# Linear attention into a two-layer network: w_in loaded in 128-row blocks, units 8 to 15 of the first tile worked block by block, and v's casts and part of q's normalisation moved to other engines

## The chip, the cores and the metric

The kernel runs on one core of a Trainium2 chip. The metric is device time in microseconds: the median of the runs, and beside it one profiled execution whose trace is read here. The engines are called TensorE (PE), VectorE (DVE), ScalarE (ACT), GpSimd (POOL) and SyncE (SP); each works through its own instructions in order and waits on semaphores for the others. DMAs are issued by SP (the hardware queue) and by POOL (the software queue, which casts f32 to bf16 on the way).

## The reference

Inputs q, k, v are (8, 8, 576, 64): batch, heads, sequence, head size. The weights are w_in (512 x 2048) and w_out (2048 x 512), all f32.

```python
q_s = softmax(q, axis=-1)            # over the 64 of a head
k_s = softmax(k, axis=2)             # over the sequence
kv  = einsum('bhsd,bhse->bhde', k_s, v)
x   = einsum('bhsd,bhde->bhse', q_s, kv)      # -> (4608 tokens, 512)
h   = x @ w_in                       # 4608 x 2048
out = maximum(0.01 * h, h) @ w_out   # 4608 x 512
```

## The kernel before

A batch has 4608 / 8 = 576 tokens. On load, one partition holds 9 consecutive rows of a head pair's sequence (R = 9; L = 64 partitions make a head), with HL = 4 such groups side by side, so a raw tile is 128 x 4 x 9 x 64 f32. `RA` are rows 0 to 3, `RB` the rest; `R1` and `R2` cut RB for the first batch. For a batch the kernel finds k's maximum over the sequence, subtracts it and takes exp (`k_tree`, `k_sub`, `k_exp`), casts v to bf16 with a column of ones (`v_cast`), multiplies both on PE (`kv`, `kv_pair`; the ones column gives the softmax denominator), and scales the result into the block-diagonal `kd`. q is shifted, exponentiated and normalised (`q_sub`, `q_exp`, `q_sum`, `q_norm`), turned on PE or by a DMA (`q_transpose`, `q_turn`), copied (`q_keep`) and multiplied by kd (`attend`) into `xT`, the network's input, turned: 4 blocks of 128 channels by 4608 tokens in bf16.

The network runs over 9 tiles of 512 tokens. Layer 1 has 16 units j per tile: a unit multiplies the 4 blocks of w_in for 128 of the 2048 inner channels with xT (`layer1`, block order 0, 2, 1, 3) and ScalarE applies the leaky function (`leaky`, into `gj`). Layer 2 (`layer2`) accumulates over the 16 blocks of w_out; `store` copies and writes out. Tile 0 is special: layer 1 goes in two halves of 256 tokens, the first half begun on units 0 to 7 with only blocks 0 and 2 (`begun`), because the x of blocks 1 and 3 is made meanwhile; its layer 2 walks j in the outer loop, 4 token groups in the inner.

The order of all engines' work is written out by hand (a manual schedule). Attention work of the next batch is hung between units with `at(tile, unit, functions)` and called by `run(tile, unit)`; units 0 to 15 are the first half's layer 1 of tile 0, 16 to 31 the second half's, 32 to 47 the w_out blocks of its layer 2.

Batch 0 at the start is written out separately. q's first four rows, k, v and q's remaining rows are loaded by SP in this order. `q_first` makes their maxima and, on ACT, 16 small exps with sums; the maxima of k go over PE (`k_max_pe`, `k_all_pe`) so that the subtraction `k_sub_ps` has one operand in PSUM. `wake(n)` puts n filler matmuls on PE.

Two kinds of lines order the transfers:

- A one-element GpSimd copy into `gate` that reads a tile holds back what is behind it on POOL's queue until that tile is there. Before, one gate on the last element of k (L516) stands ahead of the first half of w_in, another ahead of the second half (L542), behind k's last subtraction; a third (L572), on batch 1's k, stands ahead of w_out.
- `hold_sync(i, src)` (L511) is a tiny SP DMA from a corner of a weight tile; SP waits there until that piece of the weights has landed. Hold 0 stands ahead of batch 1's k, q, v; hold 1 ahead of batch 2's (`load_all(2)`).

`load_w_in(fh)` loads one half of w_in's columns with four DMAs from POOL; each takes 64 partitions for two blocks. `load_w_out` loads blocks of w_out, in pieces 0:2, 2:4, 4:8, 8:12 and 12:16.

PSUM has 6 banks under one tag for everything but the layer-2 outputs; a new tile takes a bank whose last reader is done.

Of the kernel before, what the change touches and what calls it, by code (L numbers as in the profile page):

```python
# [8 lines left out]
FP32 = mybir.dt.float32  # L9
# [10 lines left out]
L = 64  # L20
# [5 lines left out]
def kernel(  # L26
# [57 lines left out]

    ALLH, ALLR = slice(0, HL), slice(0, R)
    RA, RB = slice(0, 4), slice(4, R)
    R1, R2 = slice(4, 6), slice(6, R)
    st = [{} for _ in range(B)]


# [33 lines left out]


    w_in_r = moe_w_in.rearrange("(gg hp hh d) f -> gg hp d hh f", gg=2, hp=2, hh=2)
    w_in_t = w_in_sb.rearrange("p (hh gg) f -> p gg hh f", gg=2)

    def load_w_in(fh):
        fs = slice(fh * (F // 2), (fh + 1) * (F // 2))  # L130
        for gg in range(2):
            for hp in range(2):
                nc.gpsimd.dma_start(  # L133
                    out=w_in_t[hp * D : (hp + 1) * D, gg, :, fs], in_=w_in_r[gg, hp, :, :, fs]
                )

    w_out_r = moe_w_out.rearrange("(fb f) o -> f fb o", f=P)
# [11 lines left out]
    def k_tree(b, hs, steps=slice(0, 4)):  # L149
        n = hs.stop - hs.start  # L150
        ks = st[b]["k"][:, hs]
        if steps.start == 0:
            st[b]["t4"] = mx_pool.tile([P, HL, 4, D], FP32, name="t4")[:, 0:n]
        t4 = st[b]["t4"]
        t2, t1 = t4[:, :, 0:2], t4[:, :, 0]
        for o, i0, i1 in (
            (t4, ks[:, :, 0:4], ks[:, :, 4:8]),
            (t2, t2, t4[:, :, 2:4]),
            (t1, t1, t4[:, :, 1]),
            (st[b]["kmax"][:, hs], t1, ks[:, :, 8]),  # L160
        )[steps]:
            nc.vector.tensor_tensor(out=o, in0=i0, in1=i1, op=ALU.max)  # L162
# [46 lines left out]
    def v_cast(eng, b, gg):  # L209
        o = vb2[b % 2][:, :, gg, 0:128].rearrange("p r (h d) -> p h r d", h=2)  # L210
        i = st[b]["v"][:, 2 * gg : 2 * gg + 2]
        if eng is nc.scalar:
            eng.copy(out=o, in_=i)
        else:
            eng.tensor_copy(out=o, in_=i)  # L215
# [12 lines left out]
    def q_first(b, rs):  # L228

        n = rs.stop - rs.start  # L230
        st[b]["nmax"] = nmax = small_pool.tile([P, HL, n], FP32, name="nmax")
        qsum = small_pool.tile([P, n, HL], FP32, name="qsum")
        for hs in (slice(0, 2), slice(2, 4)):
# [12 lines left out]
        st[b]["qsum"] = qsum

    def q_first_rec(b, rs):
        n = rs.stop - rs.start
        st[b]["qrec", rs.start] = qrec = small_pool.tile([P, n, HL], FP32, name="qrec")  # L250
        nc.vector.reciprocal(out=qrec, in_=st[b]["qsum"])
# [25 lines left out]
    def q_norm(b, rs):  # L277
        n = rs.stop - rs.start
        qes = st[b]["qe"][:, rs]
        nc.vector.tensor_tensor(  # L280
            out=qes,
            in0=qes,
            in1=st[b]["qrec", rs.start].unsqueeze(3).to_broadcast([P, n, HL, D]),
            op=ALU.mult,
        )
# [256 lines left out]
    nc.gpsimd.tensor_copy(out=gate[:, 0:1], in_=st[0]["k"][:, HL - 1, R - 1, D - 1 : D])  # L542
    load_w_in(1)
    k_exp(0, H1)
    q_first_rec(0, RA)
    q_norm(0, RA)
    kv_pair(0, 0)
    wake(4)
    q_transpose(0, 0, 4)
    kv_pair(0, 1)  # L550
    for hh in range(2):
        kd_rec(0, 0, hh)
        kd_one(nc.vector, 0, 0, hh)
    q_keep(nc.scalar, 0, 0, 4, slice(0, 4, 2))
    q_keep(nc.vector, 0, 0, 4, slice(1, 4, 2))
    attend(0, [0, 2], 0, 256, nc.scalar)
    wake(3)
    kd_rec(0, 1, 0)
    kd_rec(0, 1, 1)
    kd_one(nc.vector, 0, 1, 0)  # L560
    kd_one(nc.vector, 0, 1, 1)
    q_max(0, R1)
    q_sub(nc.gpsimd, 0, R1)
    q_max(0, R2)
    q_sub(nc.gpsimd, 0, R2)
# [16 lines left out]
    at(0, 13, lambda: q_transpose(0, 6, 3), lambda: q_keep(nc.vector, 0, 6, 3))
    at(0, 15, lambda: attend(0, [0, 2], 256, 256, nc.scalar))
    at(0, 15, lambda: attend(0, [1, 3], 256, 256, nc.vector))
    at(0, 17, lambda: attend(0, [0, 1, 2, 3], 512, 64, nc.scalar))
# [3 lines left out]
    at(0, 15, lambda: q_max(1, RB), lambda: q_sub(nc.gpsimd, 1, RB))
    at(0, 29, lambda: k_exp(1, H1))  # L590
    at(0, 31, lambda: v_cast(nc.scalar, 1, 0), lambda: k_exp(1, H0))
    at(0, 33, lambda: q_exp(1, RA), lambda: q_sum(1, RA), lambda: q_norm(1, RA))
    at(0, 33, lambda: v_cast(nc.scalar, 1, 1), lambda: q_exp(1, RB), lambda: q_sum(1, RB))
# [58 lines left out]
    begun = []
    for j in range(0, 8, 2):
        ph = psB_pool.tile([P, 2, 256], FP32, name="ph", tag=BANK_TAG)
        for i in range(2):
            layer1(j + i, ph[:, i], 0, 256, slice(0, 2), i == 0)
        begun.append(ph)
    attend(0, [1, 3], 0, 256, nc.scalar)
    for half in range(2):
        for j in range(0, NF, 2):  # L660
            part = slice(2, 4) if begun else slice(0, 4)
            ph = begun.pop(0) if begun else psB_pool.tile([P, 2, 256], FP32, name="ph", tag=BANK_TAG)
            for i in range(2):
                layer1(j + i, ph[:, i], 256 * half, 256, part, i == 0, i == 1)
                if i == 1:
                    leaky(g_sb[j // 2][:, :, 256 * half : 256 * half + 256], ph)
                run(0, 16 * half + j + i)
# [65 lines left out]
```

## Time and profile before

| what | value |
|---|---|
| runs (3) | median 293.24 us, 293.17 to 293.56 |
| profiled execution | 293.27 us |
| its span, first to last instruction | 291.5 us |
| granted TensorE clock | 1.00 in every slice |
| PE busy | 280.2 us (96%) |
| DVE / ACT / POOL busy | 147.0 / 149.7 / 85.5 us |
| DMA, mean over the span | 157 GB/s; 45.76 MB |
| the chain that ended last | PE 89%, DMA 3%, DVE 1%, issue 1%, ACT 1%, POOL 1% |
| w_in pieces (8) | 256 KB each as written, 6.7 us median from issue to landing |
| w_out pieces (2 and 3) | 256 KB and 512 KB; 8.5 and 13.2 us from issue to landing |

The span is what lies between the first and the last instruction; the time is 1.8 us longer. A busy PE is not PE at its peak, because matmuls are pipelined: the view of the timeline gives the start of each group and, in brackets, the idle time before it with what ended it. In the timeline a line shows start, duration, engine, line of the kernel, operation, output and inputs, and xN for N merged instructions. Of a DMA the timeline shows only the issue; its landing is another figure. In the table by stretches each engine's busy time is followed by its instruction count, and the last columns are the granted clock, the share of the transfer engines and GB/s. The share can go over 1, because an engine's packets overlap.

### The profile page before, as it was taken

The numbers are of one execution on the slowest core, as the hardware profiler recorded it, in microseconds if no ns is written. First come the engines' busy times: TensorE is split into PE (matmuls) and PEld (weight loads), VectorE is DVE, ScalarE is ACT, GpSimd is POOL, SyncE is SP. The second block draws the span as 40 slices with busy tenths as digits, with TensorE's granted clock in tenths as the row PEclk, the third lists the DMA queues.
The fourth block names the chain that finished last, engine by engine and source line by source line (L and its number), as shares of the span: only waits on it lengthen the run. The fifth ranks groups of instructions, "written<-read, shape, count | busy, mean of one in ns | idle before, by whom it ended". The sixth has DMA issues, their size and how long they took to land.

```text
span 291.5 us, 4277 instructions
## 1 busy us (share of the span) xinstructions
PE 280.2 (96%) x1645; PEld 139.9 (48%) x1672; DVE 147.0 (50%) x244; ACT 149.7 (51%) x268; POOL 85.5 (29%) x61
## 2 busy tenths in 40 slices
PE   8697999999999999999999999999999999999995
PEld 3265845444544544454444544554455444444443
DVE  2947957896790796289276546645541200110011
ACT  4957683568168506941684339533953066017400
POOL 4545280008039208703910391029200000000000
PEclk9999999999999999999999999999999999999999
DMA  7999999597639454973299139913141310131032
GB/s 255 314 202 378 256 176 397 139 286 270 124 89 338 162 119 108 336 211 86 65 338 250 36 72 318 287 36 74 36 81 38 72 36 1 38 75 33 0 73 73
DMA packets 36580, 45.76 MB, mean 157 GB/s; under 512 B 15952, under 2 KB 19280, under 8 KB 36560
## 3 DMA queue, kind: packets, MB, share of 16 engines
q1 hardware_dynamic: 33120, 41.16, 48.4%
q0 software_dynamic: 3280, 4.20, 8.3%
q8 instruction: 13, 0.21, 0.3%
q10 hardware_dynamic: 160, 0.13, 0.1%
q14 instruction: 7, 0.06, 0.1%
HBM read 36.70 MB, written 9.44 MB: 158 GB/s over the span
## 4 chain that ended last, share of the span: by engine, by line
PE 89%; DMA 3%; DVE 1%; issue 1%; ACT 1%; POOL 1%; ACTq 0%
PE pout L479 43%; PE ph L458 41%; DMA w_in_sb<-in_moe_w_in_dram 3%; PE pkv L295 3%; PE po L446 2%; DVE k_raw L362 1%; PE psum_qt L395 1%; POOL w_in_sb L133 0%; ACT gj L467 0%; ACT xT L428 0%; PE po L418 0%; DVE out_sb L473 0%; POOL gate L542 0%; ACTq L467 0%
## 5 line engine op out<-in xcount | busy, mean ns | idle before, releaser
L479 PE MATMUL pout<-w_out_sb,gj 128*128 128x512 bf16 (+2 forms) x580 | 129.6, 373 | 0.6
L458 PE MATMUL ph<-xT,w_in_sb 128*128 128x512 bf16 (+1 forms) x626 | 126.8, 357 | 3.4 <-ACT xT L428 1.4
L467 ACT ACTIVATE gj<-ph 128x512 bf16<-128x512 f32 x144 | 82.5, 603 | 58.1 <-PE ph L458 57.5
L458 PEld LDWEIGHTS <-w_in_sb 128*128 128x128 bf16 x640 | 62.1, 98 | 64.8 <-issue 4.1
L479 PEld LDWEIGHTS <-gj 128*128 128x128 bf16 x592 | 57.0, 98 | 62.1 <-ACT gj L467 0.4
L473 DVE COPY out_sb<-pout 128x512 f32<-128x512 f32 (+1 forms) x34 | 22.7, 675 | 86.2 <-PE pout L479 80.7
L195 POOL TENSOR_TENSOR k_raw<-k_raw,kall 128x2304 f32<-128x2304 f32 (+1 forms) x6 | 29.1, 4846 | 83.5 <-DVE kall L187 56.3
L273 DVE TENSOR_REDUCE qsum<-qe 128x36 f32<-128x2304 bf16 (+4 forms) x11 | 19.8, 1799 | 37.4 <-ACT qe L264 37.4
L256 POOL TENSOR_TENSOR q_raw<-q_raw,qmax 128x2304 f32<-128x2304 f32 (+4 forms) x11 | 31.1, 2839 | 25.4 <-DVE qmax L226 25.4
L452 ACT CAST xT<-po 128x320 bf16<-128x320 f32 (+1 forms) x48 | 16.8, 402 | 41.2 <-PE po L446 41.2
L203 ACT ACTIVATE ke<-k_raw 128x2304 bf16<-128x2304 f32 (+2 forms) x11 | 17.6, 1596 | 10.3 <-POOL k_raw L195 8.6
L280 DVE TENSOR_TENSOR qe<-qe,qrec 128x2304 bf16<-128x2304 bf16 (+4 forms) x12 | 21.7, 1811 | 0.4
L226 DVE TENSOR_REDUCE qmax<-q_raw 128x36 f32<-128x2304 f32 (+4 forms) x11 | 19.4, 1789 | 0.0
L264 ACT ACTIVATE qe<-q_raw 128x2304 bf16<-128x2304 f32 (+4 forms) x11 | 16.9, 1533 | 0.8 <-POOL q_raw L256 0.8
L215 POOL CAST vb<-v_raw 128x1152 bf16<-128x1152 f32 x12 | 13.5, 1153 | 0.0
L324 PE MATMUL pout<-zero 128*128 128x512 bf16 x29 | 9.6, 470 | 1.5 <-POOL zero L101 1.3
L162 DVE TENSOR_TENSOR t<-k_raw 128x1024 f32<-128x1024 f32 (+1 forms) x10 | 10.1, 1011 | 0.5 <-DMA k_raw<-in_k_dram 0.2
L162 DVE TENSOR_TENSOR t<-t 128x256 f32<-128x256 f32 (+2 forms) x20 | 9.6, 478 | 0.7
L446 PE MATMUL po<-qX,kd 128*128 128x320 bf16 (+1 forms) x48 | 9.8, 286 | 0.0
L473 ACT COPY out_sb<-pout 128x512 f32<-128x512 f32 (+1 forms) x3 | 1.7, 563 | 14.9 <-PE pout L479 14.9
L295 PEld LDWEIGHTS <-ke 64*128 64x128 bf16 x252 | 7.2, 93 | 3.0 <-ACT gj L467 1.7
L313 DVE TENSOR_TENSOR kd<-pkv,krec 64x128 bf16<-64x128 f32 x28 | 8.1, 289 | 0.7
(57 smaller groups left out, 104.8 us busy)
## 6 DMA issues: line engine op xcount, KB each, us to landing
out_dram<-out_sb SPq DMA_DIRECT2D x70, 128.0 KB, 2.4
q_raw<-in_q_dram SPq DMA_DIRECT2D x7, 1152.0 KB, 8.4
v_raw<-in_v_dram SPq DMA_DIRECT2D x7, 1152.0 KB, 11.4
k_raw<-in_k_dram SPq DMA_DIRECT2D x6, 1152.0 KB, 6.1
k_raw<-in_k_dram SPq DMA_DIRECT2D x4, 576.0 KB, 5.7
w_in_sb<-in_moe_w_in_dram POOLq DMA_DIRECT2D x8, 256.0 KB, 6.7
w_out_sb<-in_moe_w_out_dram POOLq DMA_DIRECT2D x3, 512.0 KB, 13.2
v_raw<-in_v_dram SPq DMA_DIRECT2D x2, 576.0 KB, 7.7
```

The costliest lines, as they stand in the source:

```text
L162: nc.vector.tensor_tensor(out=o, in0=i0, in1=i1, op=ALU.max)
L195: eng.tensor_tensor(out=ks, in0=ks, in1=st[b]["kall"][:, hs].unsqueeze(2).to_broadcast([P, n, R, D]), op=ALU.subtract,)
L203: nc.scalar.activation(out=st[b]["ke"][:, :, hs].rearrange("p r h d -> p h r d"), in_=st[b]["k"][:, hs], func=AF.Exp,)
L226: nc.vector.tensor_reduce(out=m, in_=st[b]["q"][:, :, rs], axis=AX.X, op=ALU.max)
L256: eng.tensor_tensor(out=qs, in0=qs, in1=st[b]["qmax", rs.start].unsqueeze(3).to_broadcast([P, HL, n, D]), op=ALU.subtract,)
L264: nc.scalar.activation(out=st[b]["qe"][:, rs].rearrange("p r h d -> p h r d"), in_=st[b]["q"][:, :, rs], func=AF.Exp,)
L273: nc.vector.reduce_sum(out=qsum, in_=st[b]["qe"][:, rs], axis=AX.X)
L280: nc.vector.tensor_tensor(out=qes, in0=qes, in1=st[b]["qrec", rs.start].unsqueeze(3).to_broadcast([P, n, HL, D]), op=ALU.mult,)
L458: nc.tensor.matmul(ph, lhsT=w_in_sb[:, cb, j * P : (j + 1) * P], rhs=xT[:, cb, c0 : c0 + n], start=(i == 0 and first), stop=(i == NB - 1 a ...
L467: nc.scalar.activation(out=o, in_=ph, func=AF.Prelu, alpha=LEAKY_SLOPE)
L473: copy(out=out_sb, in_=pout)
L479: nc.tensor.matmul(pout, lhsT=g_sb[j // 2][:, j % 2, tsub * P : (tsub + 1) * P], rhs=w_out_sb[:, j, os], start=(j == 0), stop=(j == NF - 1),)
```

## The change

- Loads: `load_w_in` takes one 128-row block per DMA, in the order 0, 2, 1, 3 in which layer 1 uses them. The gate ahead of the second half reads `kmax` instead of the subtracted k, and v's two casts and the first normalisation now stand between that gate and the four DMAs on POOL's queue. Hold 0 reads block 2 instead of block 0. One w_out piece (0:2) goes ahead of the gate on batch 1's k, and 4:8 is cut into 4:6 and 6:8; all w_out loads and batch 2's loads are issued from the hook after unit 0.
- q of batch 0, rows 0 to 3: sums, reciprocals, normalisation, turn and copy by head pair. GpSimd normalises the first pair, VectorE the second. `attend` for blocks 0 and 2 is split in two, around the second kv product.
- q of batch 0, rows 4 to 8: rows 4 and 5 (R1), 6 and 7 (R2) earlier, with R1's normalisation on GpSimd and the turns between blocks of units 8 to 15; row 8 (R3) later, its turn and attend in layer 2 (units 35 and 38).
- Tile 0, first half: `begin` works a group of four bank pairs block by block and `end` finishes unit by unit. Units 0 to 7 begin with blocks 0 and 2, with blocks 1 and 3 of x made after block 0; units 8 to 15 with blocks 0, 2 and 1, and only block 3 is left to the unit loop.
- Batch 1's ScalarE work (exps and v's casts) stands at units 31 and 32 instead of 29 to 33. Filler matmuls go from 5, 4 and 3 to 3 and 3.

The core of the diff:

```diff
     def load_w_in(fh):
         fs = slice(fh * (F // 2), (fh + 1) * (F // 2))
         for gg in range(2):
-            for hp in range(2):
+            for hh in range(2):
                 nc.gpsimd.dma_start(
-                    out=w_in_t[hp * D : (hp + 1) * D, gg, :, fs], in_=w_in_r[gg, hp, :, :, fs]
+                    out=w_in_sb[:, 2 * hh + gg, fs], in_=w_in_r[gg, :, :, hh, fs]
                 )
...
+    def q_first_norm(eng, b, gg):
+        qes = st[b]["qe"][:, RA, 2 * gg : 2 * gg + 2]
+        eng.tensor_tensor(
+            out=qes,
+            in0=qes,
+            in1=st[b]["qrec2", gg].unsqueeze(3).to_broadcast([P, RA.stop, 2, D]),
+            op=ALU.mult,
+        )
...
     k_tree(0, H1, slice(1, 4))
+    nc.gpsimd.tensor_copy(out=gate[:, 0:1], in_=st[0]["kmax"][:, HL - 1, D - 1 : D])
+    v_cast(nc.gpsimd, 0, 0)
     k_max_pe(0, 1)
     wake(1)
     k_sub_ps(0, 0, HA)
     k_exp(0, slice(0, 1))
     k_all_dve(0, 1)
     k_all_pe(0, 1)
-    wake(5)
+    wake(3)
+    q_first_rec(0, 0)
+    q_first_norm(nc.gpsimd, 0, 0)
+    v_cast(nc.gpsimd, 0, 1)
     k_sub_ps(0, 0, HB)
     k_exp(0, slice(1, 2))
-    v_cast(nc.scalar, 0, 0)
-    v_cast(nc.scalar, 0, 1)
+    q_first_rec(0, 1)
+    load_w_in(1)
     k_sub_ps(0, 1)
-    nc.gpsimd.tensor_copy(out=gate[:, 0:1], in_=st[0]["k"][:, HL - 1, R - 1, D - 1 : D])
-    load_w_in(1)
     k_exp(0, H1)
-    q_first_rec(0, RA)
-    q_norm(0, RA)
     kv_pair(0, 0)
-    wake(4)
-    q_transpose(0, 0, 4)
+    q_turn_first(0, 0)
+    wake(3)
+    kd_rec(0, 0, 0)
+    kd_one(nc.vector, 0, 0, 0)
+    q_keep_first(nc.vector, 0, 0)
+    kd_rec(0, 0, 1)
+    kd_one(nc.vector, 0, 0, 1)
+    q_first_norm(nc.vector, 0, 1)
+    attend(0, [0], 0, 256, nc.scalar)
     kv_pair(0, 1)
+    attend(0, [2], 0, 256, nc.scalar)
+    q_turn_first(0, 1)
+    q_keep_first(nc.scalar, 0, 1)
...
-    hold_sync(0, w_in_sb[0:1, 0, F - 128 : F])
+    for rs in (R1, R2):
+        q_max(0, rs)
+        q_sub(nc.gpsimd, 0, rs)
+    hold_sync(0, w_in_sb[0:1, 2, F - 128 : F])
     st[1]["k"] = load(k, 1, "k_raw", [(H0, ALLR), (H1, ALLR)])
     st[1]["q"] = load(q, 1, "q_raw", [(ALLH, ALLR)])
     st[1]["v"] = load(v, 1, "v_raw", [(ALLH, ALLR)])
-    nc.gpsimd.tensor_copy(out=gate[:, 0:1], in_=st[1]["k"][:, 0, 0, 0:1])
-    for j0, j1 in ((0, 2), (2, 4), (4, 8), (8, 12), (12, 16)):
-        load_w_out(slice(j0, j1))
-    hold_sync(1, w_out_sb[0:1, 11, 0:128])
-    load_all(2)
+    def behind_first_units():
+        load_w_out(slice(0, 2))
+        q_max(0, R3)
+        q_sub(nc.gpsimd, 0, R3)
+        nc.gpsimd.tensor_copy(out=gate[:, 0:1], in_=st[1]["k"][:, 0, 0, 0:1])
+        for j0, j1 in ((2, 4), (4, 6), (6, 8), (8, 12), (12, 16)):
+            load_w_out(slice(j0, j1))
+        hold_sync(1, w_out_sb[0:1, 11, 0:128])
+        load_all(2)
...
+    at(0, 0, lambda: q_exp(0, R1), lambda: q_sum(0, R1), lambda: q_norm(0, R1, nc.gpsimd), behind_first_units)
+    at(0, 2, lambda: q_exp(0, R2), lambda: q_sum(0, R2), lambda: q_norm(0, R2))
+    at(0, 16, lambda: q_exp(0, R3))
+    at(0, 35, lambda: q_transpose(0, 8, 1), lambda: q_keep(nc.scalar, 0, 8, 1))
+    at(0, 38, lambda: attend(0, [0, 1, 2, 3], 512, 64, nc.scalar))
...
+    def begin(js, parts):
+        phs = [psB_pool.tile([P, 2, 256], FP32, name="ph", tag=BANK_TAG) for _ in js]
+        for i, between in parts:
+            for j, ph in zip(js, phs):
+                for h in range(2):
+                    layer1(j + h, ph[:, h], 0, 256, slice(i, i + 1), h == 0, False)
+            for fn in between:
+                fn()
+        return phs
...
+    def x1():
+        attend(0, [1], 0, 256, nc.scalar)
+        attend(0, [3], 0, 256, nc.vector)
+    t1 = (lambda: q_transpose(0, 4, 2), lambda: q_keep(nc.scalar, 0, 4, 2))
+    t2 = (lambda: q_transpose(0, 6, 2), lambda: q_keep(nc.vector, 0, 6, 2))
+    x2 = (
+        lambda: attend(0, [0, 2], 256, 256, nc.scalar),
+        lambda: attend(0, [1, 3], 256, 256, nc.vector),
+    )
+    for j0, parts in ((0, ((0, (x1,)), (1, ()))), (8, ((0, t1), (1, t2), (2, x2)))):
+        js = range(j0, j0 + 8, 2)
+        for j, ph in zip(js, begin(js, parts)):
+            end(j, ph, 0, slice(len(parts), 4), False)
+    for j in range(0, NF, 2):
+        end(j, psB_pool.tile([P, 2, 256], FP32, name="ph", tag=BANK_TAG), 1, slice(0, 4), True)
```

More of the change, by code (lines that the diff above doesn't have):

```diff
@@ L86 @@
     RA, RB = slice(0, 4), slice(4, R)
-    R1, R2 = slice(4, 6), slice(6, R)
+    R1, R2, R3 = slice(4, 6), slice(6, 8), slice(8, R)
     st = [{} for _ in range(B)]
@@ L126 @@
     w_in_r = moe_w_in.rearrange("(gg hp hh d) f -> gg hp d hh f", gg=2, hp=2, hh=2)
-    w_in_t = w_in_sb.rearrange("p (hh gg) f -> p gg hh f", gg=2)
     def load_w_in(fh):
@@ L231, in q_first @@
         st[b]["nmax"] = nmax = small_pool.tile([P, HL, n], FP32, name="nmax")
-        qsum = small_pool.tile([P, n, HL], FP32, name="qsum")
-        for hs in (slice(0, 2), slice(2, 4)):
+        for gg in range(2):
+            hs = slice(2 * gg, 2 * gg + 2)
+            st[b]["qsum", gg] = qsum = small_pool.tile([P, n, 2], FP32, name="qsum2")
             nc.vector.tensor_reduce(
@@ L236, in q_first, with q_first_rec, q_turn_first, q_keep_first @@
             )
-            for h in range(hs.start, hs.stop):
+            for h in range(2):
                 for r in range(n):
                     nc.scalar.activation(
-                        out=st[b]["qe"][:, rs.start + r, h],
-                        in_=st[b]["q"][:, h, rs.start + r],
+                        out=st[b]["qe"][:, rs.start + r, 2 * gg + h],
+                        in_=st[b]["q"][:, 2 * gg + h, rs.start + r],
                         func=AF.Exp,
-                        bias=nmax[:, h, r : r + 1],
+                        bias=nmax[:, 2 * gg + h, r : r + 1],
                         accum_out=qsum[:, r, h : h + 1],
                     )
[L246 to L251, printed above, removed]
+    def q_first_rec(b, gg):
+        st[b]["qrec2", gg] = qrec = small_pool.tile([P, RA.stop, 2], FP32, name="qrec2")
+        nc.vector.reciprocal(out=qrec, in_=st[b]["qsum", gg])
+    def q_first_norm(eng, b, gg):
[6 more added lines that the diff above has]
+        )
+    def q_turn_first(b, gg):
+        n = RA.stop
+        ps = psB_pool.tile([P, 2, n, L], BF16, name="psum_q2", tag=BANK_TAG)
+        for r in range(n):
+            nc.tensor.matmul(
+                ps[:, :, r],
+                lhsT=st[b]["qe"][:, r, 2 * gg : 2 * gg + 2].rearrange("p h d -> p (h d)"),
+                rhs=ident,
+                is_transpose=True,
+                start=(r == 0),
+                stop=(r == n - 1),
+            )
+        st[b]["ps2", gg] = ps
+    def q_keep_first(eng, b, gg):
+        o, i = st[b]["qT"][:, gg::2, RA], st[b]["ps2", gg]
+        if eng is nc.scalar:
+            eng.copy(out=o, in_=i)
+        else:
+            eng.tensor_copy(out=o, in_=i)
     def q_sub(eng, b, rs):
@@ L275, in q_sum, with q_norm @@
         nc.vector.reciprocal(out=qrec, in_=qsum)
-    def q_norm(b, rs):
+    def q_norm(b, rs, eng=nc.vector):
         n = rs.stop - rs.start
         qes = st[b]["qe"][:, rs]
-        nc.vector.tensor_tensor(
+        eng.tensor_tensor(
             out=qes,
@@ L535 @@
     k_all_pe(0, 1)
-    wake(5)
+    wake(3)
+    q_first_rec(0, 0)
+    q_first_norm(nc.gpsimd, 0, 0)
+    v_cast(nc.gpsimd, 0, 1)
     k_sub_ps(0, 0, HB)
     k_exp(0, slice(1, 2))
-    v_cast(nc.scalar, 0, 0)
-    v_cast(nc.scalar, 0, 1)
+    q_first_rec(0, 1)
+    load_w_in(1)
     k_sub_ps(0, 1)
-    nc.gpsimd.tensor_copy(out=gate[:, 0:1], in_=st[0]["k"][:, HL - 1, R - 1, D - 1 : D])
-    load_w_in(1)
     k_exp(0, H1)
-    q_first_rec(0, RA)
-    q_norm(0, RA)
     kv_pair(0, 0)
-    wake(4)
-    q_transpose(0, 0, 4)
+    q_turn_first(0, 0)
[7 more added lines that the diff above has]
+    attend(0, [0], 0, 256, nc.scalar)
     kv_pair(0, 1)
+    attend(0, [2], 0, 256, nc.scalar)
+    q_turn_first(0, 1)
+    q_keep_first(nc.scalar, 0, 1)
     for hh in range(2):
[L552 to L565, printed above, removed]
-    hold_sync(0, w_in_sb[0:1, 0, F - 128 : F])
+        kd_rec(0, 1, hh)
+        kd_one(nc.vector, 0, 1, hh)
+    for rs in (R1, R2):
+        q_max(0, rs)
+        q_sub(nc.gpsimd, 0, rs)
+    hold_sync(0, w_in_sb[0:1, 2, F - 128 : F])
     st[1]["k"] = load(k, 1, "k_raw", [(H0, ALLR), (H1, ALLR)])
@@ L582 @@
[L582 to L585, printed above, removed]
-    at(0, 15, lambda: k_begin(1), lambda: q_begin(1), lambda: k_tree(1, H0), lambda: k_tree(1, H1))
-    at(0, 15, lambda: k_allmax(1), lambda: k_sub(nc.gpsimd, 1, H0), lambda: k_sub(nc.vector, 1, H1))
-    at(0, 15, lambda: q_max(1, RA), lambda: q_sub(nc.gpsimd, 1, RA))
@@ L589 @@
[L589 to L593, printed above, removed]
+    def behind_first_units():
[7 more added lines that the diff above has]
+        load_all(2)
@@ new lines @@
+    at(0, 0, lambda: q_exp(0, R1), lambda: q_sum(0, R1), lambda: q_norm(0, R1, nc.gpsimd), behind_first_units)
[3 more added lines that the diff above has]
+    at(0, 38, lambda: attend(0, [0, 1, 2, 3], 512, 64, nc.scalar))
+    at(0, 15, lambda: k_begin(1), lambda: q_begin(1), lambda: k_tree(1, H0), lambda: k_tree(1, H1))
+    at(0, 15, lambda: k_allmax(1), lambda: k_sub(nc.vector, 1, H1), lambda: k_sub(nc.gpsimd, 1, H0))
@@ L594 @@
+    at(0, 16, lambda: q_sum(0, R3), lambda: q_norm(0, R3))
+    at(0, 16, lambda: q_max(1, RA), lambda: q_sub(nc.gpsimd, 1, RA))
+    at(0, 16, lambda: q_max(1, RB), lambda: q_sub(nc.gpsimd, 1, RB))
+    at(0, 31, lambda: k_exp(1, H1), lambda: k_exp(1, H0), lambda: v_cast(nc.scalar, 1, 0))
+    at(0, 32, lambda: q_exp(1, RA), lambda: q_sum(1, RA), lambda: q_norm(1, RA))
+    at(0, 32, lambda: v_cast(nc.scalar, 1, 1), lambda: q_exp(1, RB), lambda: q_sum(1, RB))
     at(0, 41, lambda: kv(1))
@@ L651, with end @@
     g_sb = g_tiles()
[L652 to L667, printed above, removed]
+    def begin(js, parts):
+        phs = [psB_pool.tile([P, 2, 256], FP32, name="ph", tag=BANK_TAG) for _ in js]
+        for i, between in parts:
+            for j, ph in zip(js, phs):
+                for h in range(2):
+                    layer1(j + h, ph[:, h], 0, 256, slice(i, i + 1), h == 0, False)
+            for fn in between:
+                fn()
+        return phs
+    def end(j, ph, half, part, first):
+        for h in range(2):
+            layer1(j + h, ph[:, h], 256 * half, 256, part, first and h == 0, h == 1)
+            if h == 1:
+                leaky(g_sb[j // 2][:, :, 256 * half : 256 * half + 256], ph)
+            run(0, 16 * half + j + h)
+    def x1():
[6 more added lines that the diff above has]
+        lambda: attend(0, [1, 3], 256, 256, nc.vector),
+    )
+    for j0, parts in ((0, ((0, (x1,)), (1, ()))), (8, ((0, t1), (1, t2), (2, x2)))):
[4 more added lines that the diff above has]
+        end(j, psB_pool.tile([P, 2, 256], FP32, name="ph", tag=BANK_TAG), 1, slice(0, 4), True)
     pout = [psO_pool.tile([P, O], FP32, name="pout") for _ in range(2)]
```

3 lines of the change are left out of this document (removed).

## The prediction, made before the changed kernel was run

> **What bounds the kernel now.** The page says TensorE (PE) is busy 280.2 of 291.5 us at full granted clock, so I looked only for time that PE loses. The chain of waits in order of time shows it at the front:
>
> ```profile
> 14.94 8.36 DMA w_in_sb<-in_moe_w_in_dram
> ...
> 23.44 1.69 PE ph L458 x14
> ...
> 36.41 8.37 PE pout L479 x38
> ...
> 53.30 2.10 PE ph L458 x9
> ```
>
> From 53.30 (tile 1) to 288 PE is busy 233.4 of 234.7 us by the busy table, and the diff touches nothing there. So the question is how much earlier than 53.30 tile 1 starts; that many us come off the total. The PE timeline shows what stands between:
>
> ```profile
> 17.37 1.91 PE L458 MATMUL ph<-xT,w_in_sb 128*128 128x256 bf16 x16
> 20.16 2.13 PE L458 MATMUL ph<-xT,w_in_sb 128*128 128x256 bf16 x18 [0.67 <-ACT xT L428]
> 23.44 1.69 PE L458 MATMUL ph<-xT,w_in_sb 128*128 128x256 bf16 x14 [1.15 <-DMA w_in_sb<-in_moe_w_in_dram]
> ```
>
> Unit 8 stops in its third block until the whole second half of w_in has landed (23.3). The busy table by stretches shows why that is late:
>
> ```profile
> 10.00:12.00 2.00, 1.67 (x11) 0.63 (x10) 2.00 (x5) 1.92 (x10) 0.84 (x2) 1.00 1.10 346
> ...
> 14.00:16.00 2.00, 1.82 (x31) 1.23 (x28) 1.29 (x5) 1.93 (x3) 1.57 (x3) 1.00 1.13 211
> ...
> 20.00:22.00 2.00, 1.84 (x17) 1.65 (x17) 0.00 (x0) 1.32 (x4) 0.59 (x1) 1.00 1.09 210
> 22.00:24.00 2.00, 0.85 (x9) 0.54 (x8) 1.50 (x3) 2.00 (x4) 0.00 (x0) 1.00 1.06 346
> ```
>
> The last two columns are the DMA share and GB/s: the transfer engines are full throughout, first with batch 0's q, k, v, then (about 205 GB/s written) with w_in, then with batch 1. The DMA records queue by queue put w_in's packets from 11.5 to about 22 without a gap, and batch 1 and w_out from 21.5 to 42.3. **So there are two clocks: PE's own work, and a transfer stream that is full to 42 us.** Who starts the stream's parts is in the SyncE and GpSimd timelines:
>
> ```profile
> 19.06 0.63 SPq L511 DMA_DIRECT2D held<-w_in_sb  x1
> 19.73 1.50 SPq L79 DMA_DIRECT2D k_raw<-in_k_dram  x2
> ...
> 40.62 0.52 SPq L511 DMA_DIRECT2D held<-w_out_sb  x1
> ```
>
> ```profile
> 8.28 2.57 POOL L133 DMA_DIRECT2D w_in_sb<-in_moe_w_in_dram  x4
> 13.08 0.19 POOL L542 COPY gate<-k_raw 128x1 f32<-128x1 f32 x1 [2.23 <-DVE k_raw L362]
> 13.20 2.38 POOL L133 DMA_DIRECT2D w_in_sb<-in_moe_w_in_dram  x4
> ...
> 69.79 2.24 POOL L215 CAST vb<-v_raw 128x1152 bf16<-128x1152 f32 x2
> ```
>
> The holds copy a corner of a landed piece, so their starts date landings: the fifth w_in piece at 19.0, w_out's blocks 8 to 11 at 40.6. From issue to landing, the other second-half pieces land at about 20.3, 21.7 and 23.3; w_out's pieces at 33.0, 35.1, 38.0, 40.6 and 43.1.
>
> **The change, part by part.**
>
> *v and q's first pair.* ScalarE loses two casts (2.20 us at 12.35). GpSimd is free of the first w_in issues at 10.85; gate 0.15, cast 1.12 (half of the 2.24 row) to 12.15, norm, cast. A bf16 normalisation on GpSimd is not in the trace; the nearest rows are its f32 subtraction of the same 512 elements (1.04 us) and VectorE's own normalisation of 512 (0.69). I take 1.04, and 0.69 to 2.1 (doubled) as ends. The second half's w_in issues then start at 14.4 (14.0 to 15.4), 1.2 us later than 13.20. The 0.69 normalisation of the second pair stays on VectorE at about 15.2, behind two scaled copies; one reciprocal (0.2) goes ahead of each k subtraction that follows, moving k's last exp from 14.45 to about 13.65, since ScalarE is free. The first kv product starts on k's second exp, about 12.75 instead of 13.54; the second on the last exp at 14.85 instead of 15.66. Two filler matmuls before and four after go (0.22 each), filling gaps only.
>
> *Units 0 to 7.* Attend 0, turn and keep of the second pair (0.35 + 0.6) and the copies of kd put the first layer-1 matmul at about 16.25 instead of 17.37. Sixteen matmuls, x1's two attends and the other 16 at 0.109 us are 3.9 us; blocks 3 and 4 landed by 17.8. Block 3 of x waits for VectorE, whose copy is now queued behind q's two maxima (0.68 each): 0.4 us. Units 0 to 7 end at 20.25 instead of about 22.1.
>
> *Units 8 to 15 by blocks.* Each block is 8 matmuls, 0.87 us: block 0 from 20.25 (landed 19.0; two pairs wait for ScalarE to free banks, whose queue has q's exps ahead of them) to 21.0; turn, block 2 (20.3) to 22.4; turn, block 1 (21.7) to 23.5; four attends to 23.95; block 3 (23.3) to 24.85. The q work inside costs PE what it cost before. First turn: GpSimd's normalisation of rows 4 and 5, issued behind the four w_in issues and two subtractions, is done at about 21.3, just covered; 0.5 us late costs 0.3. The second half's 64 matmuls take 6.95: layer 2 could start at 31.9, against 35.98, 4.1 us earlier. The row-8 turn and attend (0.25 + 0.28) now lie in layer 2, leaving 3.5.
>
> *The stream.* This is where the gain is cut. The blocks are 128 rows of 4 KB like the 64x2 before: same packets, no change taken (bounds none, since issue rows are 0.59 to 0.78 us for these 128 rows). The hold now waits for the sixth piece, 20.3 instead of 19.0, so k is issued at 21.0. SyncE's first packet came 1.8 us after its issue at 19.73, as w_in drained, and about 1 us after its issue at 0.74; I take 1.2, so batch 1 starts 0.3 us later than before (0 to 0.9). The w_out piece ahead of k, the gate and the extra issue (0.75; 6 issues for 5) only change the order: whatever the order, the piece with blocks 8 to 11 lands after all of batch 1 and 12 of 16 w_out blocks. So it lands at 40.6 + 0.3 = 40.9.
>
> *Layer 2.* Before, block 8's first matmul ran at 35.98 + 32 x 0.216 = 42.9 with 2.3 us in hand, and tile 1 began 10.4 us later (8 matmuls, kv of batch 1, turns, 24 matmuls, attends), unchanged in the new order. After, PE alone reaches block 8 at 31.9 + 6.9 + 0.5 = 39.3, and the piece lands at 40.9. Earlier waits (blocks 4 and 5 at about 36.3 against a need at 35.9) vanish in this one. v of batch 1 lands at 35 to 37; from there cast, exp, cast (1.14 + 1.06 + 1.14) fit before kv at 42.6. Tile 1 starts at 40.9 + 10.4 = 51.3: 2.0 us earlier.
>
> The profiled execution took 293.27 (span 291.5 plus 1.8), like the median of 293.24. **293.2 - 2.0 = 291.2 us.** Under 0.6 us, 0.2%, cannot be told from no change.
>
> **Rivals.**
>
> *The w_in stream gets a hole (about 292.6).* From the start of GpSimd's issue to the first packet passed 3.3 us at 8.28 and 3.8 at 25.23. If that is a fixed delay, pieces issued at 14.4 start at 17.7 to 18.2, while the first half runs out at 16.7: 1.0 to 1.5 us of nothing, and everything behind is as much later: 51.3 + 1.3 = 52.6, 292.5. Against it: both first packets came just when a batch transfer ran out (11.5: the last q rows; 29.0: q of batch 1), and the hardware queue's at 21.5 just when w_in did. So the delay looks like a turn awaited, with about 0.7 us in hand. [...]
>
> *GpSimd is slowed by VectorE and the kernel is slower (about 294).* In the trace GpSimd's 1152-element subtraction took 3.74 us beside VectorE's subtraction of the same size, half of the 5.07 us for twice the size being 2.5; and VectorE was held in turn:
>
> ```profile
> 34.89 3.74 POOL L195 TENSOR_TENSOR k_raw<-k_raw,kall 128x1152 f32<-128x1152 f32 x1 [5.95 <-DVE kall L187]
> ```
>
> ```profile
> 71.25 2.12 DVE L280 TENSOR_TENSOR qe<-qe,qrec 128x1280 bf16<-128x1280 bf16 x1
> ```
>
> (1.49 for that shape at 46.13; the two GpSimd casts ran until 72.0.) If the casts and norm run at half speed, 3.4 us become 6.8, the issue starts at 17.8, the stream stops for 2.8 us, and tile 1 starts at 54.1: 294.0. It decides from an issue at about 17. Against it: in that stretch VectorE subtracts with one operand in PSUM; the slow pairs have both in SBUF. [...]
>
> *PE is the only clock (289.8).* If the stream closes up where batch 1 and w_out alternate, tile 1 starts at 49.7 to 50.
>
> *The new order gives nothing*: only if PE's early start is fully lost in ScalarE's in-order queue; within the hole's result.
>
> **How the numbers follow.** Forecast 0.56 (own range 290.3 to 292.4), hole 0.15, slowed GpSimd 0.19, PE alone 0.10. The range goes from 289.7 to 294.0. Faster takes the forecast, PE alone and a little of the hole: 0.68. Same takes most of the hole, 0.13; slower 0.19.
>
> **What would show it.** Right: second w_in issue near 14.4 with DMA share full at 17 to 18, first layer-1 matmul near 16.3, layer 2 near 32, PE waiting on w_out before block 8 at about 41, tile 1 near 51.3. Wrong: issue after 16, a dip in GB/s at 17, PE waiting on kv of batch 1 instead of w_out, or a later stage that no longer starts as much earlier as tile 1 does.

## The result: 305.8 us, slower, and the profile after

The median went from 293.21 us to **305.81 us** (4 runs of each, 305.36 to 306.04 after), a ratio of 1.0425 with the interval 1.0407 to 1.0443. The profiled execution took 306.04 us, its span 304.3, its mean granted clock 0.981. The prediction, 291.2 with a range to 294.0, was wrong in size and in sign.

The forecast named the start of tile 1 as the figure that carries the time. That reading holds: tile 1 started at 53.30 before and starts at 66.07 now, 12.8 us later, and the time is 12.6 us longer. Everything lost is lost ahead of that point. Here is the PE timeline of the kernel after (start, duration, engine, line, operation; in brackets the idle time before and what ended it):

```profile
16.02 0.40 PE L264 MATMUL psum_q<-ident,qe 128*128 128x128 bf16 x4
22.17 1.89 PE L486 MATMUL ph<-xT,w_in_sb 128*128 128x256 bf16 x8 [5.75 <-DMA w_in_sb<-in_moe_w_in_dram]
...
44.99 1.89 PE L507 MATMUL pout<-w_out_sb,gj 128*128 128x512 bf16 x8 [2.32 <-DMA w_out_sb<-in_moe_w_out_dram]
...
53.01 0.28 PE L446 MATMUL po<-qT,kd 128*128 128x64 bf16 x4 [3.43 <-ACT qT L438]
53.12 4.43 PE L507 MATMUL pout<-w_out_sb,gj 128*128 128x512 bf16 x12
...
66.07 2.10 PE L486 MATMUL ph<-xT,w_in_sb 128*128 128x512 bf16 x9
```

PE was ready for layer 1 at 16.4, near the forecast 16.25, and then stood still for 5.75 us because the first piece of w_in was not there. Layer 2 waits once for w_out. The third large wait is at the row-8 attend, for a copy on ScalarE. The last number to see is 4.43 us for 12 matmuls that take 2.75 elsewhere. The busy table by stretches explains that, and the late w_in too (the last three columns are granted clock, DMA share, GB/s):

```profile
14.00:16.00 2.00, 1.95 (x27) 1.14 (x27) 1.78 (x6) 0.77 (x2) 2.00 (x3) 1.00 0.56 101
...
20.00:22.00 2.00, 0.00 (x0) 0.00 (x0) 0.00 (x0) 0.00 (x0) 0.25 (x1) 0.50 0.96 166
22.00:24.00 2.00, 1.83 (x9) 1.34 (x10) 0.00 (x0) 0.00 (x0) 0.00 (x0) 0.50 1.30 147
24.00:26.00 2.00, 2.00 (x12) 1.36 (x9) 1.15 (x3) 0.90 (x2) 0.00 (x0) 0.50 1.19 120
...
54.00:56.00 2.00, 2.00 (x6) 0.69 (x5) 1.93 (x3) 0.00 (x0) 0.00 (x0) 0.51 0.99 371
```

At 14 to 16 us, where w_in had the transfer engines to itself, they are half busy and move 101 GB/s; before it was 1.13 and 211. With the stops of 5.75 and 3.43 us the granted clock goes to half, from 19.9 to 26.7 us and from 54.0 to 57.4. Two more lines of the page, from the queues and from the DMA issues, say what is different about w_in:

```profile
q0 software_dynamic: 10464, 4.22, 9.8%
...
w_in_sb<-in_moe_w_in_dram POOLq DMA_DIRECT2D x8, 256.0 KB, 14.2
```

In the first line stand packets, MB and the share of the 16 engines' time. The software queue carried 3,280 packets before and 10,464 now, for the same 4.2 MB, and a piece takes 14.2 us to land where it took 6.7.

### The profile page after: what moved, and what is told of

Its sections match the earlier page's. It is cut to its first block, busy times and chain, and to the rows that moved or that the text cites. A ratio compares the mean times of both kernels' runs of the same rounds, so it can differ in the third digit from the quotient of the medians.

```text
span 304.3 us, 4299 instructions
## 1 busy us (share of the span) xinstructions
PE 284.7 (94%) x1666; PEld 140.8 (46%) x1666; DVE 148.1 (49%) x248; ACT 148.2 (49%) x270; POOL 92.6 (30%) x67
## 3 DMA queue, kind: packets, MB, share of 16 engines
q0 software_dynamic: 10464, 4.22, 9.8%
## 4 chain that ended last, share of the span: by engine, by line
PE 81%; DMA 8%; POOL 4%; DVE 3%; issue 1%; ACT 1%; SPq 1%; DVEq 0%
PE pout L507 40%; PE ph L486 37%; DMA w_in_sb<-in_moe_w_in_dram 5%; DMA k_raw<-in_k_dram 4%; PE pkv L323 3%; PE po L474 2%; POOL q_raw L284 1%; POOL w_in_sb L132 1%; DVE t L161 1%; POOL vb L214 1%; DVE k_raw L194 0%; ACT qe L292 0%; DVE qmax L225 0%; PE psum_qt L423 0%; SPq L79 0%
## 5 line engine op out<-in xcount | busy, mean ns | idle before, releaser
L486 PE MATMUL ph<-xT,w_in_sb 128*128 128x512 bf16 (+1 forms) x640 | 129.5, 362 | 6.8 <-DMA w_in_sb<-in_moe_w_in_dram 6.7
L507 PE MATMUL pout<-w_out_sb,gj 128*128 128x512 bf16 (+2 forms) x592 | 132.5, 377 | 2.3 <-DMA w_out_sb<-in_moe_w_out_dram 2.3
L486 PEld LDWEIGHTS <-w_in_sb 128*128 128x128 bf16 x640 | 63.0, 99 | 69.7 <-DMA w_in_sb<-in_moe_w_in_dram 7.6
L301 DVE TENSOR_REDUCE qsum<-qe 128x36 f32<-128x2304 bf16 (+4 forms) x12 | 19.9, 1661 | 34.6 <-ACT qe L292 34.6
L202 ACT ACTIVATE ke<-k_raw 128x2304 bf16<-128x2304 f32 (+2 forms) x11 | 17.6, 1597 | 14.1 <-POOL k_raw L194 10.2
L214 POOL CAST vb<-v_raw 128x1152 bf16<-128x1152 f32 x14 | 15.8, 1155 | 0.0
L352 PE MATMUL pout<-zero 128*128 128x512 bf16 x24 | 8.6, 500 | 1.3 <-POOL zero L101 1.3
L456 ACT CAST xT<-po 128x256 bf16<-128x256 f32 (+2 forms) x9 | 3.5, 409 | 12.5 <-PE po L446 12.5
## 6 DMA issues: line engine op xcount, KB each, us to landing
w_in_sb<-in_moe_w_in_dram POOLq DMA_DIRECT2D x8, 256.0 KB, 14.2
```

Source lines behind the costliest of these rows:

```text
L202: nc.scalar.activation(out=st[b]["ke"][:, :, hs].rearrange("p r h d -> p h r d"), in_=st[b]["k"][:, hs], func=AF.Exp,)
L301: nc.vector.reduce_sum(out=qsum, in_=st[b]["qe"][:, rs], axis=AX.X)
L486: nc.tensor.matmul(ph, lhsT=w_in_sb[:, cb, j * P : (j + 1) * P], rhs=xT[:, cb, c0 : c0 + n], start=(i == 0 and first), stop=(i == NB - 1 a ...
L507: nc.tensor.matmul(pout, lhsT=g_sb[j // 2][:, j % 2, tsub * P : (tsub + 1) * P], rhs=w_out_sb[:, j, os], start=(j == 0), stop=(j == NF - 1),)
```

## The experiments

Theories: **L**, the form of the new w_in DMAs slows the stream; **R**, row 8's turn and attend in layer 2 wait behind batch 1's work on ScalarE; **G**, GpSimd's casts and norm delay the second half's issue or run slowly beside VectorE; **H**, the hold on the sixth piece and the gate ahead of w_out put batch 1 and w_out at the wrong time.

**a1: the new order with the old loads.**

```diff
-            for hh in range(2):
+            for hp in range(2):
...
-    out=w_in_sb[:, 2 * hh + gg, fs], in_=w_in_r[gg, :, :, hh, fs]
+    out=w_in_t[hp * D : (hp + 1) * D, gg, :, fs], in_=w_in_r[gg, hp, :, :, fs]
```

> The changed kernel with w_in loaded as before (four DMAs of 64 partitions by two blocks per half), all else as changed. Theory A (the 128-row DMA form itself: its source has an outer dimension of 2, and its data lie on a few of the 16 transfer engines): the software queue is back to about 3,300 records (10,464 in the changed kernel), the last w_in piece lands near 23 us instead of about 32, PE's 5.8 us wait at 16.4 is gone, and the time falls from 305.8 to 290.5 to 292.5 (the lower end is the 291.2 forecast; the upper end keeps a wait of about 1.5 us for the row-8 copy, which stands on ScalarE behind batch 1's casts and exps). Theory B (GpSimd's casts, its later w_in issue, or the moved work behind it are to blame): the time stays at 300 or more, with the second half's issue near 14.5 and PE still waiting several us.

Measured: 296.89 us (294.44 to 297.68), ratio 1.0108 (1.0064 to 1.0153). 8.9 us of the loss are gone, and tile 1 starts at 57.21, 8.86 earlier than after. The queue line reads

```profile
q0 software_dynamic: 3296, 4.20, 8.1%
```

so the 7,168 extra packets belong to the new form of the DMA. What is still slower than before stands in the PE timeline and the stretch behind it:

```profile
43.01 0.37 PE L447 MATMUL po<-qT,kd 128*128 128x64 bf16 x4 [3.51 <-ACT qT L439]
43.19 5.31 PE L508 MATMUL pout<-w_out_sb,gj 128*128 128x512 bf16 x12
```

```profile
44.00:46.00 2.00, 2.00 (x6) 0.73 (x5) 1.93 (x3) 0.00 (x0) 0.00 (x0) 0.50 1.03 378
```

That is R. The wait is 3.51 us, and the half clock after it stretches 12 matmuls from 2.75 to 5.31. The runs of this one kernel part by the same clock: 294.44 us with a granted clock of 1.0 over the span, 296.6 to 297.7 with 0.987 to 0.992. ScalarE's own timeline shows what the copy stood behind:

```profile
40.10 1.14 ACT L213 CAST vb<-v_raw 128x1152 bf16<-128x1152 f32 x1
41.43 1.27 ACT L293 ACTIVATE qe<-q_raw 128x1280 bf16<-128x1280 f32 x1 [0.18 <-POOL q_raw L285]
42.60 0.35 ACT L439 COPY qT<-psum_qt 128x256 bf16<-128x256 bf16 x1
```

The copy is third in a row of batch 1's v cast and q exp, put on the queue from units 31 and 32, ahead of unit 35; the exp in turn waits for GpSimd's subtraction (c2 shows what holds that up).

**b1: before, with the new loads alone.** a1's edit the other way, in the kernel before.

> The kernel before with nothing but the changed kernel's 128-row w_in DMAs. Theory A: w_in's landings go from 14.4 to 23.3 to about 22 to 31, PE waits some 5 us before its first layer-1 matmul and several more before unit 8, batch 1 and w_out come about 9 us later; time 301 to 307. Theory B: within 1 us of 293.2.

Measured: 300.41 us, ratio 1.0243 (1.0222 to 1.0265); 10,448 packets. L alone costs 7.0 us in the old order:

```profile
22.94 0.40 PE L458 MATMUL ph<-xT,w_in_sb 128*128 128x256 bf16 x1 [5.61 <-DMA w_in_sb<-in_moe_w_in_dram]
```

**a2: 128 rows per DMA that follow each other in memory**, so that the source's slowest dimension is 128 and not 2.

```diff
+                cb = 2 * hh + gg
...
-    in_=w_in_r[gg, :, :, hh, fs]
+    in_=moe_w_in[cb * P : (cb + 1) * P, fs]
```

> The changed kernel, but each 128-row block is read from 128 consecutive rows of w_in, so the channels are permuted and the output is not the reference's; bytes, destinations (128 partitions, one block), issues and order are those of the changed kernel. Only the source's shape differs: one dimension of 128 rows instead of 2 x 64. Theory A (the outer dimension of 2 in the source): 16-engine transfers again, no 4-byte records beyond 16 per DMA, the fifth piece lands near 19, time 290.5 to 292.5. Theory A2 (128 partitions as destination, or pieces of one block, are slow in themselves): 4-byte records and late landings stay, time 304 to 306. Theory B: 300 or more with landings on time.

Measured: 296.84 us, ratio 1.0123 (1.0071 to 1.0174), and 3,296 packets. So 128 rows in a piece cost nothing here (a1 takes 296.89); the source in two parts does (305.81 after). Layer 2 started at 31.46, ahead of a1's 32.82, but the lead was lost behind it:

```profile
37.22 2.40 PE L508 MATMUL pout<-w_out_sb,gj 128*128 128x512 bf16 x8 [3.87 <-DMA w_out_sb<-in_moe_w_out_dram]
```

Here the hold waits for the sixth piece; batch 1's k was issued at 21.83 (19.73 before), the gate opened at 28.14 (24.76 before) and the second w_out piece was late. So was the piece with blocks 8 to 11, which the second hold dates:

```profile
43.40 0.52 SPq L540 DMA_DIRECT2D held<-w_out_sb  x1
```

That is H, and the clock fell behind this stop too (0.61 and 0.53 from 38 to 42). In a1 the same corner of block 2 lands with the fifth piece, and H didn't show.

**a3: each block as two DMAs of 64 partitions.**

```diff
+    for hp in range(2):
+        nc.gpsimd.dma_start(out=w_in_sb[hp * D : (hp + 1) * D, 2 * hh + gg, fs],
+                            in_=w_in_r[gg, hp, :, hh, fs])
```

> The changed kernel with each 128-row block loaded by two DMAs of 64 partitions, in the same block order: eight issues per half instead of four. Theory A: all 16 engines again; w_in ends near 22.5; but GpSimd issues until about 13.1 instead of 10.9, so v's cast and the first kv product come about 2 us later and the second half's issues start near 16.5. PE's start is later by about 1.5 us, covered at least in part by the wait for w_out: 291 to 294. Theory B: 300 or more.

Measured: 299.15 us (296.29 to 300.34), ratio 1.0185 (1.0125 to 1.0245), above the expected 291 to 294. Its 3,424 packets are a1's 3,296 and 16 for each of the eight DMAs more. The profiled run is the fastest, 296.29. In it eight issues take GpSimd 4.35 us, and the casts behind them made the first kv product wait 1.64; the clock fell with that stop:

```profile
13.75 1.16 PE L401 MATMUL pkv<-vb,ke 64*128 64x129 bf16 x18 [1.64 <-POOL vb L216]
```

```profile
14.00:16.00 2.00, 1.78 (x23) 1.35 (x19) 1.02 (x4) 0.12 (x1) 2.00 (x3) 0.50 1.13 207
```

The second half's issues took from 15.68 to 19.9, and the stream thinned: 101 to 150 GB/s from 16 to 24 us. The row-8 attend waited 2.77 for its copy, which the expectation had left out.

**c1: a1 with row 8 back among rows 6 to 8.**

```diff
-    R1, R2, R3 = slice(4, 6), slice(6, 8), slice(8, R)
+    R1, R2 = slice(4, 6), slice(6, R)
...
-    at(0, 35, ...turn and keep of row 8...)
-    at(0, 38, lambda: attend(0, [0, 1, 2, 3], 512, 64, nc.scalar))
+    at(0, 17, lambda: attend(0, [0, 1, 2, 3], 512, 64, nc.scalar))
...
-    t2 = (lambda: q_transpose(0, 6, 2), lambda: q_keep(nc.vector, 0, 6, 2))
+    t2 = (lambda: q_transpose(0, 6, 3), lambda: q_keep(nc.vector, 0, 6, 3))
```

> The kernel of a1 (changed kernel, w_in loaded as before) with row 8 of q taken back to rows 6 and 7: turned between blocks of units 8 to 15 and attended after unit 17, as before the change. Theory C (a1's 3.5 us of idle PE ahead of the row-8 attend comes from the copy standing in ScalarE's queue behind batch 1's exps and casts, and the half clock after it costs some 2.5 us more): both are gone, layer 2 starts near 33, PE meets the landing of w_out's blocks 8 to 11 (about 40.5) and tile 1 starts near 51 instead of 57.2: 290.5 to 292. Theory D (PE would have waited as long for batch 1's v, casts and kv anyway, and the row-8 wait only comes first): the wait moves to kv of batch 1 and the time stays within 1.5 us of 296.9.

Measured: **291.20 us** (291.00 to 291.48), ratio 0.9925 (0.991 to 0.994). It is 0.7% faster than the kernel before, and 5.69 us faster than a1, the whole price of R. The PE timeline from layer 2 on:

```profile
33.66 7.24 PE L508 MATMUL pout<-w_out_sb,gj 128*128 128x512 bf16 x32
41.11 1.89 PE L508 MATMUL pout<-w_out_sb,gj 128*128 128x512 bf16 x8 [0.21 <-DMA w_out_sb<-in_moe_w_out_dram]
...
51.52 2.75 PE L487 MATMUL ph<-xT,w_in_sb 128*128 128x512 bf16 x12
```

Block 8 waits for its piece at 41.1 and tile 1 starts 10.4 us later, near the forecast (40.9 and 10.4). GpSimd, with the moved casts and norm, in the same kernel:

```profile
10.98 1.18 POOL L215 CAST vb<-v_raw 128x1152 bf16<-128x1152 f32 x1
12.09 1.07 POOL L254 TENSOR_TENSOR qe<-qe,qrec 128x512 bf16<-128x512 bf16 x1
...
14.17 2.44 POOL L133 DMA_DIRECT2D w_in_sb<-in_moe_w_in_dram  x4
```

The second half is issued at 14.17, and its stream has no hole:

```profile
16.00:18.00 2.00, 1.71 (x17) 1.31 (x15) 2.00 (x4) 0.77 (x3) 1.73 (x4) 1.00 1.12 201
18.00:20.00 2.00, 1.90 (x16) 1.46 (x16) 0.89 (x2) 1.80 (x3) 1.67 (x2) 1.00 1.13 201
```

So G falls.

**c2: a1 with row 8's turn and attend later still.**

```diff
-    at(0, 35, ...turn and keep of row 8...)
+    at(0, 44, ...turn and keep of row 8...)
-    at(0, 38, lambda: attend(0, [0, 1, 2, 3], 512, 64, nc.scalar))
+    at(0, 46, lambda: attend(0, [0, 1, 2, 3], 512, 64, nc.scalar))
```

> The kernel of a1 with one thing moved: row 8's turn and copy stand at unit 44 instead of 35 and its attend at unit 46 instead of 38, behind the kv product of batch 1, when ScalarE's queue is free. Theory C: as in the run with row 8 back, 290.5 to 292, tile 1 near 51.3; no PE wait on the row-8 copy. Theory D: the wait moves to kv of batch 1, 295 to 298.

Measured: 292.70 us (291.71 to 294.53), ratio 0.9977 (0.9941 to 1.0014): no more than its equal. The wait for row 8's copy is gone and the clock stays at 1.0, which confirms R by another way; but the expected 290.5 to 292 was too good. In the profiled run (293.81) kd is late for PE (0.73 waited at 48.87), and tile 1 starts at 53.77 instead of 51.52, because batch 1's chain is 2.1 us later: the sums of its q start at 42.04 on VectorE, and at 39.92 in c1. VectorE and GpSimd show where most of that comes from:

```profile
35.62 2.19 DVE L309 TENSOR_TENSOR qe<-qe,qrec 128x256 bf16<-128x256 bf16 x1
...
39.02 4.19 POOL L285 TENSOR_TENSOR q_raw<-q_raw,qmax 128x1024 f32<-128x1024 f32 x2 [1.49 <-DVE qmax L226]
```

The normalisation of row 8 takes VectorE 2.19 us for 256 elements, where 512 took 0.69 at 20.78; it runs beside GpSimd's subtraction of batch 1's k (33.80 to 37.53). Batch 1's maxima stand behind it, and GpSimd's next subtraction waits 1.49 us for them. In c1 it does not wait; in a1 it waits 1.50. Some 0.8 us more come from batch 1's k, which landed later in this run than in c1 (gate at 27.36 and 26.36). The order of c2 doesn't explain that, because a1, with the same order up to unit 34, has its gate at 24.91.

**f1: the changed kernel with only row 8 back** (c1's edit, new loads kept).

> The changed kernel with its 128-row w_in DMAs kept, and only row 8 of q taken back to rows 6 and 7. If the two losses add: 305.8 less the 5.7 us between the runs a1 and c1, about 300.1. The changed kernel's stream says nearly the same: w_out's blocks 8 to 11 landed at 50.1, plus 10.4 us to tile 1 gives 60.5 instead of 66.1, so 300.2. Rival: with w_in late, PE waits for batch 1 anyway, the row-8 copy costs little, and the time stays above 303.

Measured: 301.10 us (300.32 to 302.05), ratio 1.0263 (1.0234 to 1.0291), below the rival's 303. R is worth 4.7 us here against 5.7 beside the old loads, and L 9.9 (f1 less c1) against 8.9 (after less a1): the two add up to within 1 us.

**f2: the changed kernel without the three losses**: a2's loads, row 8 back, and the hold on the fifth piece.

```diff
-    hold_sync(0, w_in_sb[0:1, 2, F - 128 : F])
+    hold_sync(0, w_in_sb[0:1, 0, F - 128 : F])
```

> What the forecast had assumed: the changed kernel with 128-row w_in blocks on 16 engines (read from 128 consecutive rows, so the channels are permuted and the output is not the reference's), batch 1's loads held only for the fifth piece, and row 8 back with rows 6 and 7. If the transfer stream is the clock: PE reaches layer 2 at 31.5 to 32, earlier than c1's 33.7, but waits for w_out's blocks 8 to 11 at about 41, tile 1 at 51 to 51.6, time 290.6 to 291.4, no better than c1's 291.2. If PE is the clock: 289.3 to 290.2.

The expectation calls this what the forecast had assumed. It is not quite that: the forecast has the hold on the sixth piece and row 8 in layer 2, and prices them at 0.3 and 0.5 us.

Measured: 291.09 us (290.85 to 291.65), ratio 0.9917 (0.9901 to 0.9934).

```profile
31.89 1.89 PE L508 MATMUL pout<-w_out_sb,gj 128*128 128x512 bf16 x8
35.23 1.89 PE L508 MATMUL pout<-w_out_sb,gj 128*128 128x512 bf16 x8 [1.45 <-DMA w_out_sb<-in_moe_w_out_dram]
37.45 3.61 PE L508 MATMUL pout<-w_out_sb,gj 128*128 128x512 bf16 x16 [0.34 <-DMA w_out_sb<-in_moe_w_out_dram]
41.27 1.89 PE L508 MATMUL pout<-w_out_sb,gj 128*128 128x512 bf16 x8 [0.21 <-DMA w_out_sb<-in_moe_w_out_dram]
```

Layer 2 starts 1.8 us ahead of c1's and the lead goes into waits for w_out: block 8 is at 41.27 against 41.11. Behind the w_in stage the transfer stream is the clock, as the forecast said.

**f3: a source whose slowest dimension is 4.**

```diff
-    in_=w_in_r[gg, :, :, hh, fs]
+    in_=moe_w_in.rearrange("(a b c) f -> b a c f", a=4, b=4)[cb, :, :, fs]
```

> A dose: the changed kernel with each 128-row block read from 4 groups of 32 consecutive rows 128 rows apart (rows are permuted, so the output is not the reference's); the source's outer dimension is 4 instead of 2. Theory A (the data of a DMA lie on as many engines as that dimension allows, the others write only 4-byte records): 12 idle engines x 32 records x 8 DMAs = 3,072 of them, some 6,370 records on the software queue (10,464 with 2; 3,296 with 128 in one dimension); each piece takes 4 engines about 5.5 us, the four pieces of a half run side by side on all 16, so the first lands near 18 and the last of the second half near 24; the time is a few us below 305.8 and above a2's 296.8: 297 to 301. If only a dimension of 2 or an odd shape were special: either 10,464 records again or 3,296.

Measured: 6,368 packets, some 6,370 expected, but 301.2 us, at the upper edge of what was expected (2 runs, 300.96 and 301.43; ratio 1.0265, 1.0244 to 1.0285). The first landing was expected near 18; the first layer-1 matmul ran at 21.23. Four DMAs on four engines each would fill all 16, and the share is indeed full, but not the rate:

```profile
14.00:16.00 2.00, 1.92 (x27) 1.03 (x25) 1.93 (x7) 1.14 (x4) 2.00 (x4) 1.00 1.26 150
```

Why a full share moved only 150 GB/s stays open; from 13 to 18 us the queue's 356 packets took 127.2% of the 16 engines' time, by which one took some 286 ns on average (an estimate from these two), where a 2 KB packet of the kernel before took 173 (median).

**What the packets say.** The new DMA reads a source of 2 x 64 x 1024 and writes 128 partitions. Suppose that only two engines carry the data of each DMA, 64 rows each, and the other 14 write 64 four-byte records: 8 x 14 x 64 = 7,168, the measured difference from a1. With four engines, 8 x 12 x 32 = 3,072, the difference of f3. The four DMAs of a half then use at most 8 of 16 engines, close to the share of 0.56. That fits all the counts, a2's 3,296 with nothing added as well; which engine wrote which record isn't in the trace, so it is a reading and not seen directly. The records do show that 9.0 packets of 2 KB were in flight at a time at 15 us, where 17.6 were before, and that each took 173 ns (median) in both: what fell is the number in flight, so here rows that lie apart are not slower by themselves. At 22 to 26 us the share is over 1 at 120 to 147 GB/s, because 6 to 12 of the four-byte records were in flight beside 9 to 14 of the 2 KB packets.

## Why the prediction was wrong, point by point

- **"The blocks are 128 rows of 4 KB like the 64x2 before: same packets, no change taken (bounds none [...])."** This is the step that failed most: 0 was taken, 8.9 us measured (after less a1; 7.0 in the old order, by b1). I compared sizes of rows and not the shape of the source, whose two halves are not adjacent. All of the stream's landings hung on it. The wait for w_in was 6.7 us in all (1.9 in a1). The clock fell to half behind it, and the issue of the first half took 3.37 us instead of 2.57. The hold was released at 30.47 instead of 20.3, and w_out's gate opened at 35.91. The piece with blocks 8 to 11 landed at 50.1 instead of 40.9.
- **Row 8, "0.25 + 0.28" of PE.** Here 0.5 was taken and 5.7 measured (a1 less c1; 4.7 by f1). The step counted PE's own time and forgot that the copy between turn and attend stands on ScalarE's queue. I followed the moved DMAs through their queues, and not this copy through its own. In a1's profiled run 3.5 is the wait and about 2.6 (5.31 less 2.75) the half clock that follows. VectorE was left out as well: c2, where the copy is free, is still 1.5 us above c1, and row 8's normalisation holds up batch 1 there.
- **"Batch 1 starts 0.3 us later than before (0 to 0.9)"** and **"The w_out piece ahead of k, the gate and the extra issue [...] only change the order".** Not so where the hold waits for the sixth piece: in a2 k is issued 2.1 us later than before, PE stops for 3.87 us at the second w_out piece, earlier than the stop that I had priced, and the piece with blocks 8 to 11 lands at 43.40 instead of 40.9. With the 10.4 us from there tile 1 would start at 53.8, no earlier than the 53.30 before: an estimate, since no run has this hold with w_in on time and row 8 back. By it this step alone would have used up the gain. f2, with the fifth piece, lands it at 41.25 and waits 2.0 for w_out in all; it has row 8 back too, so the hold's price is read from the landings and not from a run of its own.
- **Right, or nearly:** the first layer-1 matmul came at 15.3 to 15.6 where w_in was on time (a1, a2, c1), 0.7 to 1.0 us before the forecast.
- **Right:** GpSimd's part. The norm took 1.07 to 1.08 (1.04 taken), the casts 1.16 to 1.19 (1.12). The issue came at 13.87 in a1 and 14.17 in c1 (14.4 forecast), and at 14.99 in the kernel after, of which 0.8 is the longer first issue. The GpSimd rival falls by the cast of 1.19 at 11.80, run beside VectorE's PSUM subtraction (1.30 from 11.90); the hole by the full share of 16 to 20 us in c1 (1.12 and 1.13).
- **Right:** the stream as the clock of layer 2. PE as the only clock falls by f2's waits. That the sum of 2.0 us comes out too (c1 gives 2.2 and f2 2.4 us; in f2 layer 2 is at 31.89, 31.9 forecast, block 8 at 41.27, 40.9 forecast, and tile 1 at 51.68, 51.3 forecast) is partly luck: neither kernel is the one forecast, and both have batch 1's k issued at about 20.0, on the fifth piece, and not at 21.0.
- None of the rivals was the mechanism that made it slower: each took the pieces' own transfer as given. (The rival with the hole is headed 292.6 where its sum gives 292.5; nothing hangs on it.)

## What to carry to other kernels

Before a DMA's shape is changed, write down the slowest dimension of its source: with 2 there in place of 64 a load of the same bytes and rows fell from 211 to 101 GB/s here (by the reading above, from 16 engines to 2 for each DMA), and the packet count of its queue showed it at once (10,464 for 3,280). When a step is moved behind other work, follow it through every engine that it touches, a 0.35 us copy included, and look at what will stand ahead of it there. Look, too, at what a hold releases: one piece later cost the stream 2.5 us more than forecast. Price a long wait on TensorE with the half clock that it brings: here each one of 3.43 to 5.78 us brought 3.4 or 6.8 us of it, and in a3 one of 1.64 brought 3.4.

## What the runs showed of the hardware that was not expected

The granted TensorE clock fell to half with every stop of 3.43 us or more in the traced start of these kernels: 5.75 and 3.43 (after), 3.51 (a1), 3.87 (a2), 5.61 (b1), 5.78 (f1) and 5.31 (f3). It stayed at 1.00 over 3.17 (f3) and 2.77 (a3). But the length of one stop does not decide alone. In a3 the clock fell at 13.3 us with a stop of 1.64, and it does not fall at a fixed time: 1.9 us into the stop of 5.31 (f3), and 1.2 us after the end of that of 3.87 (a2). The stretches at half clock lasted 3.4 us (a2, a3, and the second in after) or twice that, 6.8 (the others). What decided in a3 stays open.
